# Row sums of twelve more attention pairs in groups of 16 rows, and another place for the squares of the weights

## The chip, the cores and the metric

The kernel runs on one core of a Trainium2 chip. The metric is device time in microseconds (us), the median of several executions; three executions before the change took 805.28, 805.90 and 806.34 us. The profile is of one more execution, taken by the hardware profiler.

## The reference

Three steps follow one another. The first is attention over 4 batches and 12 heads, 448 tokens, head size 64, with a soft cap on the scores:

```
scores = cap * tanh((q @ k.T / 8) / cap)
attn   = exp(scores - max);  attn = attn / sum(attn)
x      = attn @ v                                  # (4, 448, 768)
xk, xr = mu * x + (1 - mu) * x_prev                # two mixes with the token before
k      = relu(xk @ w_k);  y = sigmoid(xr @ w_r) * ((k * k) @ w_v)
theta  = y @ w_theta
u      = y + w_tok_r @ (y * cos(theta)) + w_tok_i @ (y * sin(theta))
out    = u + relu(u @ w_ch)
```

The weights arrive as 64-bit floats. The kernel turns them into float32 with shifts, finds a power-of-two scale from the sum of their squares, and splits each scaled value into two float16 parts, high and low; a large product is then three float16 matmuls.

## The kernel before, in words

**Layout.** Activations lie with features on the 128 partitions and the 448 tokens along the free side. Attention works on 24 pairs of heads, six to a batch.

**A pair.** `scores` (L633) makes the transposed scores of both heads in float32, four tiles of the array at a time (L653, L649). ScalarE applies tanh (L662) and exp (L666). Key rows 0 to 383 are three tiles `th`; the last 64 key rows are a half tile `tl`, in which the two halves of the partitions hold the two halves of the queries. VectorE adds the three full tiles into `z` (L739). Then the row sums, their reciprocals and the product with v follow, in one of two ways.

**`narrow` (L669), pairs 0 to 11.** The sums are 16 small float32 products into 32 array columns each (L676 with `z`, L680 with `tl`); sums of 16-row groups end up in eight groups on the partitions, 112 columns wide. VectorE takes the reciprocal of 128x112 (L687). Four float32 products (L692, `spread`) copy the reciprocals back over 128 partitions and 448 columns. The product with v (L698, L701) is copied out of PSUM with a scale (L703, recorded at L296 on ScalarE or L300 on VectorE), and VectorE multiplies it by the spread reciprocals, read from PSUM (L704).

**`wide` (L706), pairs 12 to 23 (`WIDE = 12`, L283).** Two additions first fold `tl` into `z` (L745). The sums are two products with a column of ones, broadcast to 64 array columns (L712), so they are on every partition at once. VectorE takes the reciprocal of 128x448 (L718), there is no spread, and one instruction scales the product with v (L724, L727) and multiplies by the reciprocals (L729).

**After a pair.** `attend` (L732) goes on to the two mixes with the token before (L751, L755), their float16 high part (L757) and low part (L758). Six finished pairs let a batch's products with w_k and w_r begin (`units`, L776, matmuls L783 to L785); they are laid between the matmuls of the next six pairs. After the last pair come the products with w_v (also L783 to L785), then the theta, token and channel products (L957 to L959, L987 to L989, L1009 to L1011).

**Weights.** `group` (L515) loads a block of raw 64-bit words into one of two buffers `w` (L380, L520, L530), rescales the exponent word (`rebase`, L451), and builds float32 in one of three buffers `f` with three VectorE steps (L461, L464, L467, the last one being `b3`). `squares` (L491) has ScalarE square `f` with a running sum (L495). The squares themselves are of no use and are written over the raw words, so `w` is in use until the square is done. A product with ones sums over partitions (L500), three tiny VectorE steps make the scale (`size`, L504), then the high part (L542) and the low part (L543) are written into the weight's tile. w_k takes its squares on the matrix engine (`grams`) and is not concerned. `tokens` (L863) does the same for the seven tiles of the two token matrices. The tile of w_theta and those of the token matrices exist once the last pair is done (`o_r2`, L852), that of w_ch once all w_k and w_r products are done (`o_l2`, L853).

**Order.** Each operation is declared with an engine, a duration, a rank and what it reads and writes. `Plan.order` (L149) runs the list through a small model with these durations and writes down one fixed order for each engine and for the DMA queue of SyncE. All engines then go through their list in that order, waiting where data is late. So a declared duration changes the order of every list after it.

Of the kernel before, what the change touches and what calls it, by code (L numbers as in the profile page):

```python
# [7 lines left out]
F32 = mybir.dt.float32  # L8
# [4 lines left out]
AF = mybir.ActivationFunctionType  # L13
ALU = mybir.AluOpType
# [4 lines left out]
B, H, S, D = 4, 12, 448, 64  # L19
# [5 lines left out]
SH = S // 2  # L25
# [5 lines left out]
KT = 7  # L31
# [217 lines left out]
def v1(n):  # L249
    return 0.17 + n / 940.0  # L250
# [6 lines left out]
def act(n):  # L257
    return 0.17 + n / 1150.0
# [19 lines left out]
def body(nc, tc, exact, qk, v, cap, mu_k, mu_r, w_k, w_v, w_r, w_th, w_tr, w_ti, w_ch, out):  # L278
    P = Plan()
    op = P.op  # L280
    ENG = {"ACT": nc.scalar, "DVE": nc.vector, "POOL": nc.gpsimd}
    SLOT = 7.9
    WIDE = 12  # L283
    WV0, WV1 = 190.0, 28.0
    WT0, WT1, WO0, WC0, WC1 = 1440.0, 10.0, 1510.0, 1660.0, 20.0
    K20, VM0, VM1 = 390.0, 1500.0, 100.0
# [21 lines left out]
    def tt(n, half=False):  # L308
        return {"POOL": pool(n) - 0.00021 * n * half, "DVE": v1(n)}
# [60 lines left out]
    def small(n=1):  # L370
        used[0] += n
        return Buf(tile=scal[:, used[0] - n:used[0]])
# [115 lines left out]
        op("PE", 0.3, rank, lambda: nc.tensor.matmul(ps.t[:, 0:1], unit[0:w].to_broadcast([w, 128]), d.t[0:w], start=True, stop=True), r=[d], w=[ps], name="bcast")  # L488
        return ps

    def squares(rank, parts, d):  # L491

        ps = Buf(c_ps)
        for a, (f, val, n, dead) in enumerate(parts):
            op("ACT", act(n) + 0.19, rank, lambda a=a, val=val, n=n, dead=dead: nc.scalar.activation(out=dead.t[:, 0:n], in_=val(), func=AF.Square, accum_out=d.t[:, a:a + 1]),  # L495
               r=[f] if f is not dead else [], w=[dead, (d, a)], name="norm")

        def total():
            for a in range(len(parts)):
                nc.tensor.matmul(ps.t[:, 0:1], unit.to_broadcast([128, 128]), d.t[:, a:a + 1], start=(a == 0), stop=(a == len(parts) - 1))  # L500
        op("PE", 0.2 + 0.1 * len(parts), rank, total, r=[d], w=[ps], name="bcast")
        return ps
# [12 lines left out]
    def group(rank, src, dst, m, inv, nb, after=(), early=False):  # L515

        sw, n = small(), 128 * nb
        vals, parts = [], []
        for a in range(len(dst)):
            w, f = Buf(w_s), Buf(f_s)  # L520
            vals.append(f)

            def half(i, w=w):
                return w.t[:, 0:2 * n].bitcast(U32).rearrange("p (n two) -> p n two", two=2)[:, :, i]

            def val(f=f):
                return f.t[:, 0:n]

            def ld(w=w, a=a):
                nc.sync.dma_start(out=w.t[:, 0:2 * n].bitcast(U32).rearrange("p (i n) -> p i n", i=nb),  # L530
                                  in_=src[n * a:n * a + n, 256 * m:256 * m + 256].rearrange("(i p) n -> p i n", p=128))
            op("DMA", 0.03 + n / 350, rank - 12, ld, w=[w], after=[o_open1], name="wld")
            bits(rank, lambda h=half: h(1), lambda h=half: h(0), val, val, n, w, f, f)
            parts.append((f, val, n, 128 if early else w))
        size(rank, grams(rank, [parts], small()) if early else squares(rank, parts, small(len(parts))), inv, m, sw)
        for a, f in enumerate(vals):
            def part(i, a=a):
                return dst[a].t[:, :, i, 128 * m:128 * m + 128]

            def val(f=f):  # L540
                return f.t[:, 0:n].rearrange("p (i n) -> p i n", i=nb)
            op({**cs(n), "DVE": (v1 if nb % 2 else v2)(n) + 0.06}, 0, rank, lambda e, val=val, part=part: copy(e, part(0), val(), sw.t), r=[f, sw], w=[(dst[a], (m, 0))], after=after, name="whi")  # L542
            grouped.append(op("DVE", v1(n) + 0.06, rank, lambda val=val, part=part: nc.vector.scalar_tensor_tensor(  # L543
                out=part(1), in0=val(), scalar=sw.t, in1=part(0), op0=ALU.mult, op1=ALU.subtract),
               r=[f, sw, (dst[a], (m, 0))], w=[(dst[a], (m, 1))], name="wlo"))
# [14 lines left out]
    for b in range(B):  # L560
        R = (2 * NP * b - 7.1) * SLOT if b else 3
        vb = v[NP * b:NP * b + NP].rearrange("g p n -> (g p n)").rearrange("(p n) -> p n", p=128)
        parts = []
        n = 2 * DM
        for c in range(2):
            t = Buf(w_s)
            op("DMA", 0.03 + n / 700, R - 10, lambda t=t, c=c, vb=vb: nc.sync.dma_start(out=t.t, in_=vb[:, c * n:(c + 1) * n]), w=[t], after=[o_open1], name="ldm")
            parts.append([(t, lambda t=t: t.t, n, 128)] if b == 0 else (t, lambda t=t: t.t, n, t))
        size(R, squares(R, parts, small(2)) if b else grams(R, parts, small()), small(), 0, sv[b])
        times(R, sv[b], qi, sx[b])  # L570
        inverse(R, sx[b], ix[b], 0.0, 2.0)
# [14 lines left out]
    last1 = []  # L586
# [79 lines left out]
            op("ACT", act(n * S) + 0.08, A + 3 + 1.8 * c, lambda th=th: nc.scalar.activation(out=th.t, in_=th.t, func=AF.Exp, scale=cap_t),  # L666
               w=[th], name="exp", table="exp")

    def narrow(A, x, sxb, th, vn, z, sp, rs, ps):  # L669

        def sums():

# [4 lines left out]
            for k in range(2):  # L677
                for h, i in ((0, 0), (0, 1), (1, 0), (1, 1)):
                    c = 32 * (2 * h + i)
                    nc.tensor.matmul(sp.t[c:c + 32, 0:SQ], ones[:, 1 + i, k], th[3].t[:, h, SQ * k:SQ * k + SQ], start=False, stop=(k == 1))  # L680
        op("PE", 0.74, A, sums, r=[z, th[3]], w=[sp], name="sums")

        def den():

# [5 lines left out]
        def spread():  # L690
            for i in range(4):
                nc.tensor.matmul(sp.t[:, SQ * i:SQ * i + SQ], live["row"][:, i].rearrange("p h d -> p (h d)"), rs.t, start=True, stop=True)  # L692
        op("PE", 0.8, A + 2, spread, r=[rs], w=[sp], name="spread")

        def av():
            for c in range(3):
# [6 lines left out]
        op({"ACT": act(S) + 0.09, "DVE": 0.7}, 0, A + 3, lambda e: copy(e, x.t[:, 1:S + 1], ps.t[:, 0:S], sxb.t), r=[ps, sxb], w=[x], name="avo")  # L703
        last1.append(op("DVE", v1(S), A + 6, lambda: nc.vector.tensor_tensor(out=x.t[:, 1:S + 1], in0=x.t[:, 1:S + 1], in1=sp.t[:, 0:S], op=ALU.mult), r=[sp], w=[x], name="norm"))  # L704

    def wide(A, x, sxb, th, vn, z, sp, ps):  # L706

        rs = lambda: x.t[:, 1:S + 1]

        def sums():  # L710
            for h in range(2):
                nc.tensor.matmul(sp.t[64 * h:64 * h + 64, 0:S], unit.to_broadcast([128, D]), z.t[:, h], start=True, stop=True, skip_group_check=True)  # L712
        op("PE", 0.74, A, sums, r=[z], w=[sp], name="sums")

        def den():
            if exact:
                nc.vector.tensor_scalar(out=rs(), in0=sp.t[:, 0:S], scalar1=1e-9, scalar2=None, op0=ALU.add)
            nc.vector.reciprocal(out=rs(), in_=rs() if exact else sp.t[:, 0:S])  # L718
        op("DVE", 2.95, A + 1, den, r=[sp], w=[x], name="den")

        def av():
            for c in range(3):
                for h in range(2):
                    nc.tensor.matmul(ps.t[64 * h:64 * h + 64, 0:S], vn.t[0][:, h, c], th[c].t[:, h], start=(c == 0), stop=False, skip_group_check=True)  # L724
            for i in range(2):
                for h in range(2):
                    nc.tensor.matmul(ps.t[64 * h:64 * h + 64, SH * i:SH * i + SH], vn.t[1][:, i, h], th[3].t[:, h], start=False, stop=True, skip_group_check=True)  # L727
        op("PE", 3.02, A + 0.5, av, r=[vn, *th], w=[ps], name="av")
        last1.append(op("DVE", v1(S) + 0.06, A + 4, lambda: nc.vector.scalar_tensor_tensor(  # L729
            out=x.t[:, 1:S + 1], in0=ps.t[:, 0:S], scalar=sxb.t, in1=rs(), op0=ALU.mult, op1=ALU.mult), r=[ps, sxb], w=[x], name="norm"))  # L730

    def attend(g):  # L732
        A = g * PAIR + 10
        th, vn = thb[g], vnb[g]
# [4 lines left out]
            op("DVE", v1(2 * S), A - 4 + i, lambda i=i: nc.vector.tensor_tensor(out=z.t, in0=th[0].t if i == 1 else z.t, in1=th[i].t, op=ALU.add),  # L739
               r=[th[0], th[1]] if i == 1 else [th[i]], w=[z], name="sum")  # L740

        if g >= WIDE:
            for i in range(2):
                p, q = slice(64 * i, 64 * i + 64), slice(SH * i, SH * i + SH)
                op(tt(S), 0, A - 1 + 0.5 * i, lambda e, p=p, q=q: e.tensor_tensor(out=z.t[p, :, q], in0=z.t[p, :, q], in1=th[3].t[p], op=ALU.add), r=[th[3]], w=[(z, i)], name="fold")  # L745
            wide(A, x, sx[b], th, vn, z, sp, ps)
        else:
            narrow(A, x, sx[b], th, vn, z, sp, rs, ps)
        R = A + 7
        d, t0 = Buf(mx_s), Buf(mx_s)  # L750
        op(tt(S), 0, R, lambda e: e.tensor_tensor(out=d.t, in0=x.t[:, 1:S + 1], in1=x.t[:, 0:S], op=ALU.subtract), r=[x], w=[d, (t0, "x")], name="mxd")  # L751
# [111 lines left out]
    def tokens(rank):  # L863
        fo = []
        for i in range(KT):
            raw, f = Buf(w_s), Buf(xf_s)
            parts = {3: ((w_tr, 384, 64, 0), (w_ti, 0, 64, 64))}.get(i, ((w_tr, 128 * i, 128, 0) if i < 3 else (w_ti, 128 * i - 448, 128, 0),))
            for src, r0, rows, p0 in parts:
                op("DMA", 0.03 + rows * S * 8 / 360e3, rank - 12, lambda src=src, r0=r0, rows=rows, p0=p0, raw=raw: nc.sync.dma_start(
                    out=raw.t[p0:p0 + rows, 0:2 * S].bitcast(U32), in_=src[r0:r0 + rows]), w=[(raw, p0)], after=[o_open1], name="wld")  # L870

            def half(j, raw=raw):
                return raw.t[:, 0:2 * S].bitcast(U32).rearrange("p (n two) -> p n two", two=2)[:, :, j]

            def fv(f=f):
                return f.t
            bits(rank, lambda h=half: h(1), lambda h=half: h(0), fv, fv, S, raw, f, f, [o_r2])
            fo.append((f, fv, S, raw))
        size(rank, squares(rank, fo, small(KT)), io, 0, so)
        tiny(rank, lambda: nc.vector.tensor_scalar(out=iw.t, in0=io.t, scalar1=2.0 ** 49, scalar2=None, op0=ALU.mult), r=[io], w=[iw])  # L880

        tiny(rank, lambda: nc.vector.tensor_scalar(out=tb.t, in0=io.t, scalar1=2.0 ** 70, scalar2=1.0, op0=ALU.mult, op1=ALU.add), r=[io], w=[tb])
# [210 lines left out]
```

## Time and profile before

| | |
|---|---|
| median of three executions | 805.9 us |
| the profiled execution | 805.84 us |
| its span, first to last instruction | 804.0 us |
| mean granted TensorE clock | 0.993 |
| busy: TensorE, VectorE, ScalarE, GpSimd | 96%, 70%, 55%, 12% |
| attention with wide sums | about 188 to 362 us |

PE is TensorE, DVE VectorE, ACT ScalarE, POOL GpSimd, SP SyncE; PEld is TensorE's weight load, and a q behind an engine's name its instruction queue, where DMAs are issued. A float32 matmul shows as two records. The recorded length of a matmul overlaps that of the next one; what a product takes of the engine's time is read from the starts of records that follow one another.

### The profile page before, as it was taken

How to read it: one execution, taken by the hardware profiler on the slowest of the kernel's cores; microseconds unless marked ns; L12 is line 12 of the kernel's file. 1: busy time of each engine (PE TensorE's matmuls, PEld its weight loads, DVE VectorE, ACT ScalarE, POOL GpSimd, SP SyncE). 2: the span in 40 equal slices, each digit the busy share in tenths (PEclk: the TensorE clock that was granted, in tenths of full speed). 3: DMA queues.
4: the chain of work that ended last, by engine and by line, in shares of the span. 5: the costliest groups of instructions: out<-in, count | busy, mean ns of one | idle time of the engine just before them, and what ended most of it. 6: DMA issues, size and time to landing. Idle time of an engine off the chain costs nothing.

```text
span 804.0 us, 12769 instructions
## 1 busy us (share of the span) xinstructions
PE 770.6 (96%) x4924; PEld 386.0 (48%) x4924; DVE 563.6 (70%) x1014; ACT 440.8 (55%) x677; POOL 92.6 (12%) x99
## 2 busy tenths in 40 slices
PE   5989999999999999998999889999999999999996
PEld 2445455454444444443555445555555555555553
DVE  2888897967778899879657768966856544645531
ACT  4889877878775875755526434355635333222201
POOL 1214403201130120101001000101201000000000
PEclk9999999999999999999999999999999999999999
DMA  8855455455343434225556866553535333324402
GB/s 258 257 173 181 158 180 191 138 171 184 113 136 99 139 92 157 97 75 172 176 191 221 296 193 203 185 152 84 123 60 136 82 92 92 90 65 98 99 28 73
DMA packets 116829, 114.76 MB, mean 143 GB/s; under 512 B 55820, under 2 KB 108824, under 8 KB 116760
## 3 DMA queue, kind: packets, MB, share of 16 engines
q1 hardware_dynamic: 116592, 113.86, 46.8%
q8 instruction: 40, 0.66, 0.3%
q14 instruction: 29, 0.24, 0.1%
q10 hardware_dynamic: 168, 0.01, 0.0%
HBM read 78.98 MB, written 23.86 MB: 128 GB/s over the span
## 4 chain that ended last, share of the span: by engine, by line
PE 87%; DMA 5%; DVE 4%; ACT 2%; issue 1%; SPq 1%; ACTq 0%; DVEq 0%
PE one L783 12%; PE one L784 11%; PE one L785 11%; PE big L653 7%; PE q L989 4%; PE q L987 4%; PE q L988 4%; PE one L724 4%; PE one L1010 3%; PE one L1009 3%; PE one L1011 3%; PE one L698 3%; PE q L957 2%; PE q L959 2%; PE q L958 2%; DMA w<-in_v 2%
## 5 line engine op out<-in xcount | busy, mean ns | idle before, releaser
L662 ACT ACTIVATE th<-big,tsc 128x896 f32<-128x896 f32 x72 | 70.1, 1002 | 22.6 <-PE big L653 22.4
L653 PE MATMUL big<-qk 64*64 64x448 f32 x576 | 67.8, 571 | 8.2 <-DMA qk<-in_qk 7.7
L783 PE MATMUL one<-k,wv 128*128 128x448 f16 x192 | 68.3, 356 | 6.2 <-DVE z L909 6.2
L666 ACT ACTIVATE th<-th,cap_t 128x896 f32<-128x896 f32 x72 | 73.0, 1039 | 0.0
L783 PE MATMUL one<-sl,wk 128*128 128x448 f16 x192 | 68.5, 357 | 2.4 <-ACT g L794 1.9
L784 PE MATMUL one<-sl,wk 128*128 128x448 f16 x192 | 68.2, 355 | 0.9 <-POOL sl L758 0.9
L784 PE MATMUL one<-k,wv 128*128 128x448 f16 x192 | 68.2, 355 | 0.0
L785 PE MATMUL one<-k,wv 128*128 128x448 f16 x192 | 68.1, 355 | 0.0
L785 PE MATMUL one<-sl,wk 128*128 128x448 f16 x192 | 68.1, 355 | 0.0
L989 PE MATMUL q<-wo,zt 128*128 128x448 f16 x168 | 59.2, 352 | 0.0
L987 PE MATMUL q<-wo,zt 128*128 128x448 f16 x168 | 59.2, 352 | 0.0
L988 PE MATMUL q<-wo,zt 128*128 128x448 f16 x168 | 59.2, 352 | 0.0
L1013 ACT ACTIVATE z<-one,scal 128x448 f32<-128x448 f32 x24 | 15.1, 627 | 71.9 <-PE one L1011 71.9
L783 PE MATMUL one<-sl,wr 128*128 128x448 f16 x144 | 50.9, 354 | 0.0
L785 PE MATMUL one<-sl,wr 128*128 128x448 f16 x144 | 50.7, 352 | 0.0
L784 PE MATMUL one<-sl,wr 128*128 128x448 f16 x144 | 50.7, 352 | 0.0
L973 DVE SCALAR_TENSOR_TENSOR cs<-xf,scal,cs 128x896 f32<-128x896 f32 x24 | 27.6, 1150 | 31.6 <-DMA xf<-xd 24.2
L718 DVE RECIPROCAL xt<-one 128x448 f32<-128x448 f32 x12 | 35.5, 2956 | 14.0 <-PE one L712 14.0
L758 POOL TENSOR_TENSOR sl<-mx,sl 128x448 f16<-128x448 f32 x24 | 29.5, 1230 | 119.2 <-ACT sl L294 100.6
L454 ACT ACTIVATE w<-w 128x768 f32<-128x768 f32 (+2 forms) x26 | 21.4, 823 | 35.0 <-DMA w<-in_w_ch 17.4
L1014 DVE TENSOR_TENSOR xf<-z,xf 128x448 f32<-128x448 f32 x24 | 15.0, 624 | 34.4 <-ACT z L1013 34.2
L991 DVE SCALAR_TENSOR_TENSOR xf<-q,scal,xf 128x448 f32<-128x448 f32 x24 | 16.4, 683 | 31.8 <-PE q L989 31.6
(191 smaller groups left out, 1739.5 us busy)
## 6 DMA issues: line engine op xcount, KB each, us to landing
qk<-in_qk SPq DMA_DIRECT2D x23, 448.0 KB, 3.8
kd<-g SPq DMA_DIRECT2D x32, 224.0 KB, 2.0
vn<-in_v SPq DMA_DIRECT2D x24, 256.0 KB, 2.7
w<-in_v SPq DMA_DIRECT2D x8, 768.0 KB, 6.2
w<-in_w_k SPq DMA_DIRECT2D x8, 768.0 KB, 5.1
w<-in_w_v SPq DMA_DIRECT2D x12, 512.0 KB, 4.4
zd<-tmp SPq DMA_DIRECT2D x24, 224.0 KB, 2.6
z<-zd SPq DMA_DIRECT2D x24, 224.0 KB, 2.9
```

The source lines that it names most:

```text
L653: nc.tensor.matmul(ps.t[o, h, 0:S], t.t[p, 1, 128 * c + 64 * i:128 * c + 64 * i + 64], t.t[p, 0], start=True, stop=True)
L662: op("ACT", act(n * S) + 0.08, A + 1 + 1.8 * c, lambda src=src, th=th: nc.scalar.activation(out=th.t, in_=src(), func=AF.Tanh, scale=tsc), ...
L666: op("ACT", act(n * S) + 0.08, A + 3 + 1.8 * c, lambda th=th: nc.scalar.activation(out=th.t, in_=th.t, func=AF.Exp, scale=cap_t), w=[th], ...
L718: nc.vector.reciprocal(out=rs(), in_=rs() if exact else sp.t[:, 0:S])
L724: nc.tensor.matmul(ps.t[64 * h:64 * h + 64, 0:S], vn.t[0][:, h, c], th[c].t[:, h], start=(c == 0), stop=False, skip_group_check=True)
L758: op(tt(S, True), 0, R + i, lambda e, t=t, hi=hi, lo=lo: e.tensor_tensor(out=lo.t, in0=t.t, in1=hi.t, op=ALU.subtract), r=[t, hi], w=[lo], ...
L783: nc.tensor.matmul(ps.t[:, 0:S], wh, xh(), start=(kk == 0), stop=False)
L784: nc.tensor.matmul(ps.t[:, 0:S], wh, xl(), start=False, stop=False)
L785: nc.tensor.matmul(ps.t[:, 0:S], wl, xh(), start=False, stop=(kk == len(xs) - 1))
L987: nc.tensor.matmul(o, z.t[:, 0, i], wo[i].t[:, 0], start=(i == 0), stop=False)
L988: nc.tensor.matmul(o, z.t[:, 1, i], wo[i].t[:, 0], start=False, stop=False)
L989: nc.tensor.matmul(o, z.t[:, 0, i], wo[i].t[:, 1], start=False, stop=(i == KT - 1))
```

## The change

All pairs take the way of `narrow`, now called `normal`; `wide` and its fold additions are gone. The declared durations of its sums and its spread are lowered, from 0.74 to 0.36 and from 0.8 to 0.47. The square of a weight block is written over the place of that block's own float16 parts instead of its raw words, and so must wait until that place exists.

```
-    WIDE = 12
...
-    def squares(rank, parts, d):
+    def squares(rank, parts, d, after=()):
...
-            op("ACT", ..., nc.scalar.activation(out=dead.t[:, 0:n], in_=val(), func=AF.Square, accum_out=d.t[:, a:a + 1]),
-               r=[f] if f is not dead else [], w=[dead, (d, a)], name="norm")
+            op("ACT", ..., nc.scalar.activation(out=place(), in_=val(), func=AF.Square, accum_out=d.t[:, a:a + 1]),
+               r=[f] if f not in dead else [], w=[*dead, (d, a)], after=after, name="norm")
...  (group)
-            parts.append((f, val, n, 128 if early else w))
-        size(rank, ... squares(rank, parts, small(len(parts))), inv, m, sw)
+            parts.append((f, val, n, 128) if early else (f, ..., n, [(dst[a], (m, 0)), (dst[a], (m, 1))],
+                          lambda a=a: dst[a].t[:, :, :, 128 * m:128 * m + 128].bitcast(F32)))
+        size(rank, ... squares(rank, parts, small(len(parts)), after), inv, m, sw)
...  (tokens)
-            fo.append((f, fv, S, raw))
+            fo.append((f, ..., S, [(wo[i], 0), (wo[i], 1)], lambda i=i: wo[i].t.bitcast(F32)))
...
-    def narrow(A, x, sxb, th, vn, z, sp, rs, ps):
+    def normal(A, x, sxb, th, vn, z, sp, rs, ps):
-        op("PE", 0.74, A, sums, r=[z, th[3]], w=[sp], name="sums")
+        op("PE", 0.36, A, sums, r=[z, th[3]], w=[sp], name="sums")
-        op("PE", 0.8, A + 2, spread, r=[rs], w=[sp], name="spread")
+        op("PE", 0.47, A + 2, spread, r=[rs], w=[sp], name="spread")
-    def wide(A, x, sxb, th, vn, z, sp, ps):
...
-        if g >= WIDE:
-            for i in range(2):
-                op(tt(S), ..., name="fold")
-            wide(A, x, sx[b], th, vn, z, sp, ps)
-        else:
-            narrow(A, x, sx[b], th, vn, z, sp, rs, ps)
+        normal(A, x, sx[b], th, vn, z, sp, rs, ps)
```

## Rows read from the trace of the kernel before

**Rows 1.** Busy time by stretch: span, then busy us of each engine, PEclk, DMA.

```profile
188.00:362.00 174.00, 173.08 (x1130) 76.31 (x1123) 145.19 (x217) 121.08 (x188) 24.62 (x21) 1.00 0.37 117
362.00:375.00 13.00, 10.12 (x47) 4.37 (x46) 11.49 (x17) 7.98 (x15) 3.59 (x3) 0.92 0.39 125
...
440.00:484.00 44.00, 36.41 (x193) 18.89 (x192) 31.55 (x73) 17.86 (x31) 2.86 (x4) 0.98 0.72 239
```

**Rows 2.** Waits of PE from 188 to 363 us: total, times, longest.

```profile
PE one L712 <- DVE xt L718: 0.9, 1, 0.9
```

**Rows 3.** Timeline of PE, a narrow pair: start, length, line.

```profile
114.96 0.59 PE L676 MATMUL one<-pz,ones 128*32 128x112 f32 x16
...
115.86 0.36 PE L783 MATMUL one<-sl,wk 128*128 128x448 f16 x1
...
118.52 0.35 PE L785 MATMUL one<-sl,wk 128*128 128x448 f16 x1
118.71 1.04 PE L692 MATMUL one<-rs,row 128*128 128x112 f32 x8
119.59 0.35 PE L783 MATMUL one<-sl,wk 128*128 128x448 f16 x1
```

**Rows 4.** Timeline of PE, the sums of a wide pair.

```profile
223.50 0.97 PE L712 MATMUL one<-pz,unit 128*64 128x448 f32 x4
224.40 0.36 PE L783 MATMUL one<-sl,wk 128*128 128x448 f16 x1
```

**Rows 5.** Chain that ended last, in time: start, us, what (two neighbourhoods).

```profile
26.07 1.07 PE one L692 x8
...
193.04 0.75 PE one L712 x4
```

**Rows 6.** Instructions by line and shape: busy us, mean ns, idle before and releaser.

```profile
L718 DVE RECIPROCAL xt<-one 128x448 f32<-128x448 f32 x12 | 35.5, 2956 | 14.0 <-PE one L712 14.0
L745 DVE TENSOR_TENSOR pz<-pz,tl 64x448 f32<-64x448 f32 x20 | 14.1, 706 | 0.5
L687 DVE RECIPROCAL rs<-one 128x112 f32<-128x112 f32 x12 | 10.2, 852 | 2.9 <-PE one L680 2.7
L729 DVE SCALAR_TENSOR_TENSOR xt<-one,scal,xt 128x448 f32<-128x448 f32 x12 | 8.2, 679 | 0.3 <-PE one L727 0.2
L704 DVE TENSOR_TENSOR xt<-xt,one 128x448 f32<-128x448 f32 x12 | 7.4, 621 | 7.0 <-PE one L692 7.0
L296 ACT ACTIVATE xt<-one,scal 128x448 f32<-128x448 f32 x9 | 5.7, 636 | 7.0 <-PE one L701 6.7
```

**Rows 7.** Waits of PE from 363 to 425 us.

```profile
PE one L783 <- ACT g L794: 1.8, 2, 1.6
PE one L784 <- POOL sl L758: 0.9, 1, 0.9
```

**Rows 8.** Waits of PE from 425 to 500 us.

```profile
PE one L783 <- DVE z L909: 6.2, 3, 2.9
```

**Rows 9.** Waits of SP's queue, whole span: total, times, longest.

```profile
SPq L530 <- ACT w L495: 43.9, 23, 4.4
```

**Rows 10.** Timeline around one load of w_ch: VectorE, ScalarE and SP.

```profile
462.59 0.95 DVE L467 SCALAR_TENSOR_TENSOR f<-w,f 128x768 uint32<-128x768 uint32 x1
...
467.08 0.83 ACT L495 ACTIVATE w<-f 128x768 f32<-128x768 f32 x1
...
467.51 0.43 SPq L950 DMA_DIRECT2D xf<-xd  x1
468.34 0.38 SPq L530 DMA_DIRECT2D w<-in_w_ch  x1
...
476.00 0.91 ACT L454 ACTIVATE w<-w 128x768 f32<-128x768 f32 x1 [5.74 <-DMA w<-in_w_ch]
```

**Rows 11.** w_theta: its low parts, and its first use (duration, first and last start).

```profile
L543 DVE SCALAR_TENSOR_TENSOR wt<-f,scal,wt x6: 1002/1008/1012, 368.9 to 400.4; 128x768 f16<-128x768 f32 x6
...
L957 PE MATMUL q<-xs,wt x96: 352/352/353, 468.9 to 734.3; 128*128 128x448 f16 x96
```

More of the change, by code (lines that the diff above doesn't have):

```diff
@@ L489, in grams @@
         return ps
-    def squares(rank, parts, d):
+    def squares(rank, parts, d, after=()):
         ps = Buf(c_ps)
-        for a, (f, val, n, dead) in enumerate(parts):
-            op("ACT", act(n) + 0.19, rank, lambda a=a, val=val, n=n, dead=dead: nc.scalar.activation(out=dead.t[:, 0:n], in_=val(), func=AF.Square, accum_out=d.t[:, a:a + 1]),
-               r=[f] if f is not dead else [], w=[dead, (d, a)], name="norm")
+        for a, (f, val, n, dead, place) in enumerate(parts):
+            op("ACT", act(n) + 0.19, rank, lambda a=a, val=val, place=place: nc.scalar.activation(out=place(), in_=val(), func=AF.Square, accum_out=d.t[:, a:a + 1]),
+               r=[f] if f not in dead else [], w=[*dead, (d, a)], after=after, name="norm")
         def total():
@@ L533, in group @@
             bits(rank, lambda h=half: h(1), lambda h=half: h(0), val, val, n, w, f, f)
-            parts.append((f, val, n, 128 if early else w))
-        size(rank, grams(rank, [parts], small()) if early else squares(rank, parts, small(len(parts))), inv, m, sw)
+            parts.append((f, val, n, 128) if early else (f, lambda val=val: val().rearrange("p (i t n) -> p i t n", i=nb, t=2), n, [(dst[a], (m, 0)), (dst[a], (m, 1))],
+                                                                     lambda a=a: dst[a].t[:, :, :, 128 * m:128 * m + 128].bitcast(F32)))
+        size(rank, grams(rank, [parts], small()) if early else squares(rank, parts, small(len(parts)), after), inv, m, sw)
         for a, f in enumerate(vals):
@@ L567, in body @@
             op("DMA", 0.03 + n / 700, R - 10, lambda t=t, c=c, vb=vb: nc.sync.dma_start(out=t.t, in_=vb[:, c * n:(c + 1) * n]), w=[t], after=[o_open1], name="ldm")
-            parts.append([(t, lambda t=t: t.t, n, 128)] if b == 0 else (t, lambda t=t: t.t, n, t))
+            parts.append([(t, lambda t=t: t.t, n, 128)] if b == 0 else (t, lambda t=t: t.t, n, [t], lambda t=t: t.t))
         size(R, squares(R, parts, small(2)) if b else grams(R, parts, small()), small(), 0, sv[b])
@@ L704, in narrow @@
         last1.append(op("DVE", v1(S), A + 6, lambda: nc.vector.tensor_tensor(out=x.t[:, 1:S + 1], in0=x.t[:, 1:S + 1], in1=sp.t[:, 0:S], op=ALU.mult), r=[sp], w=[x], name="norm"))
-    def wide(A, x, sxb, th, vn, z, sp, ps):
[L708 to L724, printed above, removed]
-            for i in range(2):
[L726 to L730, printed above, removed]
     def attend(g):
@@ L740, in attend @@
                r=[th[0], th[1]] if i == 1 else [th[i]], w=[z], name="sum")
-        if g >= WIDE:
-            for i in range(2):
-                p, q = slice(64 * i, 64 * i + 64), slice(SH * i, SH * i + SH)
-                op(tt(S), 0, A - 1 + 0.5 * i, lambda e, p=p, q=q: e.tensor_tensor(out=z.t[p, :, q], in0=z.t[p, :, q], in1=th[3].t[p], op=ALU.add), r=[th[3]], w=[(z, i)], name="fold")
-            wide(A, x, sx[b], th, vn, z, sp, ps)
-        else:
-            narrow(A, x, sx[b], th, vn, z, sp, rs, ps)
+        normal(A, x, sx[b], th, vn, z, sp, rs, ps)
         R = A + 7
@@ L877, in tokens @@
             bits(rank, lambda h=half: h(1), lambda h=half: h(0), fv, fv, S, raw, f, f, [o_r2])
-            fo.append((f, fv, S, raw))
-        size(rank, squares(rank, fo, small(KT)), io, 0, so)
+            fo.append((f, lambda f=f: f.t.rearrange("p (t n) -> p t n", t=2), S, [(wo[i], 0), (wo[i], 1)], lambda i=i: wo[i].t.bitcast(F32)))
+        size(rank, squares(rank, fo, small(KT), [o_r2]), io, 0, so)
         tiny(rank, lambda: nc.vector.tensor_scalar(out=iw.t, in0=io.t, scalar1=2.0 ** 49, scalar2=None, op0=ALU.mult), r=[io], w=[iw])
```

## The prediction

> **What bounds the kernel now.** I first read the busy time by stretch, to see which engine fills the stage that the change rewrites. In the stage with wide sums, 188 to 362 us, TensorE is busy 173.08 of 174 us at clock 1.00, VectorE 145.19 and ScalarE 121.08 [rows 1]. Busy time of overlapped matmuls can flatter, so the second view is TensorE's waits in that stage: one, of 0.9 us [rows 2]. The third is its timeline: from the product at 115.86 to the one at 118.52 are fourteen steps of 448 columns in 2.66 us, 0.19 us each [rows 3], which is 448 columns at 2.4 GHz, so nothing is left between them. TensorE bounds this stage, and what is added to its list there is added to the time, unless it fits into the few waits elsewhere. Those after the stage are at the join with the last batch, 362 to 375 us, where TensorE is idle 2.88 us at clock 0.92 [rows 1, 7], and in the w_v products, 440 to 484 us, where it waits 6.2 us for VectorE to empty a PSUM bank [rows 8].
>
> **Pairs 12 to 23, TensorE.** Removed: the wide sums. Start to next start they take 0.90 us between float16 products [rows 4], and 0.75 us where they follow the product with v, whose array shape they share [rows 5]; three of the twelve stand so in the timeline, hence a mean of (9 x 0.90 + 3 x 0.75) / 12 = 0.86 us. Added: the narrow sums, also 0.90 us (114.96 to 115.86) [rows 3]. They are 16 small products, but they stream as many columns as the wide ones, four at a time instead of two, and half of the steps are the `tl` rows, which the wide way had folded in on VectorE. Added as well: the spread, which the wide way doesn't have. It takes 0.88 us between float16 products (118.71 to 119.59) [rows 3] and 1.07 us between products of other array shapes [rows 5]. The stage is full of float16 products, so I take 0.90, near the first. A pair gains 0.90 + 0.90 - 0.86 = 0.94 us, twelve pairs 11.3 us. The bounds: 0.90 + 0.88 - 0.90 = 0.88 us, in all 10.6; and 0.90 + 1.07 - 0.75 = 1.22 us, in all 14.6. That the declared durations fall to 0.36 and 0.47 does not make the chip faster: the same instructions have the rows above.
>
> **Pairs 12 to 23, the other engines.** VectorE loses a 2.96 us reciprocal for one of 0.85, 14.1 us of fold additions, and 0.68 for 0.62 in the last product [rows 6]; over twelve pairs 25.3 + 14.1 + 0.7 = 40 us, less some 2 us for the three copies in twelve that VectorE made in the narrow pairs. ScalarE gets the other copies at 0.64 us [rows 6], some 6 us on 121 of 174. These I cost at nothing, and credit with little: TensorE covers both. Of the one wait of 0.9 us, for the long reciprocal [rows 2], all goes, as that reciprocal goes. The PSUM bank of the sums is now held through the spread to the last product, 0.90 + 0.85 + 0.90 + 0.62 = 3.3 us against 0.90 + 2.96 = 3.9 us before, so nothing is late for it; if waits lengthen that, the product with ones of a weight scale queues behind it on TensorE.
>
> **The join.** After the last pair's sums the chain was 2.96 + 0.68 us to a finished x; it becomes 0.85 + 0.90 + 0.62, so 1.3 us shorter [rows 3, 6]. Behind it stand casts and subtractions that also hold TensorE up (0.9 us for a GpSimd subtraction, 1.6 us for a ScalarE eviction [rows 7]); I credit 1.0 us. The bounds are nothing, and all 2.9 us of idle time with the 1.0 us that a clock of 0.92 costs over 13 us [rows 1].
>
> **Squares.** 23 loads wait for the square of an earlier block to free its raw words [rows 9]; now `b3` frees them. The case that matters is the load before the longest late eviction: `b3` ends at 463.54, the square starts at 467.08, the load is issued at 468.34 and lands for the rescale at 476.00 [rows 10]. But SP's list has an xf load just ahead, issued at 467.51 for 0.43 us, so with this list the gain is about 0.4 us; I take 0.4. It would be 4 us or more if the list puts the load further ahead, up to the whole 6.2 us of waits [rows 8]. Below nothing: a load issued earlier stands in SP's list ahead of loads that are wanted sooner; by the load's own 0.38 us of issue, shifted for each of 30 blocks and seven token tiles, that is 14 us of queue time in all, spread over 400 us and mostly off the path. The square writes as many bytes as before; its duration stays. It waits for its place: w_theta's blocks now start their squares after the last pair, but the last low part was written at 400.4 and first use is at 468.9 [rows 11], a cover of 68 us against a few squares of under 1 us. For w_ch the first square in the trace is behind the opening of its tile anyway.
>
> **Sum.** 805.84 (the profiled execution; 0.06 under the median of 805.9, and 1.84 over its span of 804.0) + 11.3 - 0.9 - 1.0 - 0.4 = 814.8 us.
>
> **A rule against this reading.** The trace says TensorE is full, by its waits and by the 0.19 us steps. The Trainium skill, Perfetto Trace Analysis, section Identifying the Most-Contended Engine, says that matmul busy share is a bad measure, and that weight-load busy share (with the share of peak arithmetic) should be read instead. By weight loads the stage stands at 76.31 of 174 us, 44% [rows 1], and VectorE at 83% would be the most contended; the sum would then follow VectorE, the second rival. The 0.19 us steps disagree with it in this stage.
>
> **Rivals.** *First, the late waits close.* Early-freed words and a shorter join could take all of them: 805.84 + 11.3 - 0.9 - 2.9 - 1.0 - 6.2 = 806.1 us. For it: these waits hang on in-order lists, and the lists are written anew. Against: a single list position decides each, and a transfer of some 7 us remains. Chance 0.13, around 805.5 to 809. *Second, faster: VectorE sets the pace of the wide stage,* and TensorE's matmuls stretch to fill it. Then 38 us of VectorE work leave and the 11.3 us fit into gaps. A full gain would be 805.84 - 38 = 768 us, a quarter of it 796; it decides from 11.3 us of hidden TensorE gaps on. For it: VectorE is busy 83% there, and waits 14.0 us for wide sums [rows 6]. Against: one wait of 0.9 us and steps with no gap. Chance 0.07. *Third, new waits.* The plan now declares a narrow pair 0.71 us lighter (0.74 + 0.8 less 0.36 + 0.47), against rows of 0.90 and 0.88, in all 24 pairs. VectorE's and ScalarE's lists may then hold instructions that wait for a TensorE which is behind the plan, with evictions queued behind them. One such wait costs 0.9 to 2.9 us as now [rows 2, 8]; three more of 2.9 make 823.5. Against: a plan in which TensorE is late mostly makes the others wait for it, not the reverse. Chance 0.18, from 819 up. That the change does not do what it says I see no room for.
>
> **How the numbers follow.** The forecast, chance 0.62, has its own range from 809 (10.6, with half of the late waits gone: 805.84 + 10.6 - 0.9 - 2 - 3.1 = 810.4, and a little more from the load) to 819.5 (14.6 with the 0.9 us alone gained). The range of 806 to 822 takes in most of the first rival and the lower part of the third. A measurement can tell about 0.2%, 1.6 us, from no change. Faster by more is the second rival, 0.07; within it lie those of the first under 807.4, 0.06; slower is the rest, 0.87.
>
> **What would show it.** TensorE's instructions grow by 12 x (32 + 8 - 4) = 432 records; L692 has 192 records and L676 and L680 384 each. Between about 188 and 373 us TensorE stays full with the stage some 11 us longer, while VectorE's busy time falls by near 38 us. L687 shows 24 times at 0.85 us. Waits of SP for L495 fall from 23 to few, replaced by waits for L467. The prediction is wrong if the spread takes less than 0.5 us from start to start among float16 products, if the stage with pairs 12 to 23 is not longer, or if TensorE's waits after 362 us change by more than 6 us in sum.

## The result, and the profile after

The changed kernel takes 813.12 us, the median of eight executions (809.86 to 815.58), against 805.82 us, the median of eight executions of the kernel before beside it: a ratio of 1.0084, with a 95% interval from 1.0062 to 1.0107. That is 7.3 us slower; the forecast was 9.0 us slower. The profiled execution took 813.44 us, 7.6 us more than the profiled one of before, over a span of 811.7 us.

In the file after, lines from L456 on stand one line earlier and those behind the removed function some 32 earlier: L495 is L494, L783 to L785 are L751 to L753, L794 is L762, L909 is L877.

Busy time of the profiled execution after, from the page:

```profile
PE 783.8 (97%) x5356; PEld 402.8 (50%) x5356; DVE 539.8 (67%) x1022; ACT 434.5 (54%) x660; POOL 85.0 (10%) x96
```

TensorE has 5356 matmul records where it had 4924: the 432 more that were worked out. VectorE's busy time fell by 23.8 us over the whole span (563.6 before), less than the 40 us of instructions that went, as the new order gave VectorE other operations. The stretches that answer to [rows 1], with the end of the stage moved to where the last pair now is (span, busy us of PE, PEld, DVE, ACT, POOL, then PEclk):

```profile
188.00:376.00 188.00, 188.00 (x1534) 93.60 (x1533) 122.91 (x225) 118.01 (x182) 12.40 (x13) 1.00 0.37 122
376.00:410.00 34.00, 31.52 (x166) 17.04 (x166) 28.38 (x60) 20.02 (x41) 4.22 (x4) 0.95 0.56 173
440.00:484.00 44.00, 40.53 (x211) 21.28 (x210) 34.67 (x85) 21.96 (x35) 4.11 (x5) 0.96 0.74 242
```

TensorE is full through the whole stage, while VectorE fell from 83% to 65% busy. Where TensorE still waits after the stage, which answers to [rows 7, 8]; the stage itself has no wait, so the one of [rows 2] is gone:

```profile
PE one L751 <- ACT g L762: 2.4, 2, 2.2
```

```profile
PE one L751 <- DVE z L877: 3.5, 3, 2.5
```

The first is the join, the second the w_v products. The narrow instructions by line and shape, which answer to [rows 6], and two groups of moved squares with one that still lies over its input (busy us, mean ns, idle before):

```profile
L692 PE MATMUL one<-rs,row 128*128 128x112 f32 x192 | 26.3, 280 | 1.0 <-DVE rs L687 1.0
L687 DVE RECIPROCAL rs<-one 128x112 f32<-128x112 f32 x24 | 20.5, 856 | 19.2 <-PE one L680 19.0
L704 DVE TENSOR_TENSOR xt<-xt,one 128x448 f32<-128x448 f32 x24 | 14.9, 620 | 21.5 <-PE one L692 21.4
...
L494 ACT ACTIVATE w<-w 128x1536 f32<-128x1536 f32 x6 | 8.9, 1476 | 0.6 <-DMA w<-in_v 0.6
L494 ACT ACTIVATE wr<-f 128x768 f32<-128x768 f32 x6 | 5.0, 842 | 4.8 <-DVE f L466 2.5 <-PE one L753 2.3
L494 ACT ACTIVATE wc<-f 128x768 f32<-128x768 f32 x6 | 5.0, 838 | 0.9 <-DVE wc L543 0.7
```

A square into the strided place of the float16 parts takes 838 to 842 ns; over the raw words, in the kernel before, the same shape took 836:

```profile
L495 ACT ACTIVATE w<-f 128x768 f32<-128x768 f32 x18 | 15.0, 836 | 9.3 <-issue 4.0 <-DVE f L467 3.9 <-DVE scal L511 1.4
```

So the place costs nothing in length. It does cost a wait: ScalarE stood idle for 2.3 us before the w_r squares until a w_r product was done (the row of `wr` above), and at 149.0 us a w_r product of TensorE waited 1.1 us, which the profile puts down to such a square. From 100 to 188 us this is TensorE's only wait in the changed kernel; the kernel before has no such wait:

```profile
PE one L751 <- ACT wr L494: 1.1, 1, 1.1
```

The waits of SP's queue, which answer to [rows 9], show that the loads are freed by `b3` now:

```profile
SPq L529 <- DVE f L466: 40.0, 18, 5.9
...
SPq L529 <- ACT w L494: 2.9, 2, 2.3
```

And the timeline of TensorE in a pair that was wide before, which answers to [rows 3, 4]:

```profile
304.70 0.59 PE L676 MATMUL one<-pz,ones 128*32 128x112 f32 x16
305.10 0.57 PE L680 MATMUL one<-tl,ones 128*32 128x112 f32 x16
305.60 0.36 PE L751 MATMUL one<-sl,wk 128*128 128x448 f16 x1
...
309.09 1.04 PE L692 MATMUL one<-rs,row 128*128 128x112 f32 x8
309.96 0.35 PE L751 MATMUL one<-sl,wk 128*128 128x448 f16 x1
```

Sums take 0.90 us from start to start and the spread 0.87, as in pairs 0 to 11.

**Two sums for each run.** To compare runs I split the time where the last pair's product with v starts, and end it where the last matmul starts (some 6 us without TensorE follow in every run). I take the float16 products out at 0.1886 us each, their usual step, since plans lay some of them on one side or the other. What is left ahead of that point is the attention's own TensorE time with all waits; behind it are the other small products, all waits and half-clock stretches. Of pairs 12 to 23, eleven wide sums lie ahead of that point in the kernel before, and twelve narrow sums with eleven spreads in the changed one. Before: the last pair starts at 358.7 us with 753 float16 products ahead, so 358.7 - 753 x 0.1886 = 216.7 us, and 24.2 us behind. After: 372.6 us with 765 ahead, so 228.3 us, and 20.3 us behind. The change costs 11.6 us ahead of the last pair and gives 3.9 back behind it: 7.7, as the spans differ.

### The profile page after: what moved, and what is told of

It reads as the page before. It is cut to its first block, busy times and chain, and to the rows that moved or that the text cites. A ratio compares the mean times of both kernels' runs of the same rounds, so it can differ in the third digit from the quotient of the medians.

```text
span 811.7 us, 13604 instructions
## 1 busy us (share of the span) xinstructions
PE 783.8 (97%) x5356; PEld 402.8 (50%) x5356; DVE 539.8 (67%) x1022; ACT 434.5 (54%) x660; POOL 85.0 (10%) x96
## 4 chain that ended last, share of the span: by engine, by line
PE 84%; DMA 6%; DVE 5%; ACT 3%; issue 1%; ACTq 0%; DVEq 0%; SPq 0%
PE one L751 11%; PE one L752 10%; PE one L753 10%; PE big L653 6%; PE one L698 6%; PE q L957 4%; PE q L955 4%; PE q L956 4%; PE one L977 3%; PE one L979 3%; PE one L978 3%; PE one L692 2%; PE q L925 2%; PE q L927 2%; PE q L926 2%; PE one L701 2%
## 5 line engine op out<-in xcount | busy, mean ns | idle before, releaser
L751 PE MATMUL one<-k,wv 128*128 128x448 f16 x192 | 68.3, 356 | 3.6 <-DVE z L877 3.5
L751 PE MATMUL one<-sl,wk 128*128 128x448 f16 x192 | 68.6, 357 | 2.4 <-ACT g L762 2.4
L753 PE MATMUL one<-sl,wk 128*128 128x448 f16 x192 | 68.3, 356 | 0.4 <-DVE wk L543 0.4
L753 PE MATMUL one<-k,wv 128*128 128x448 f16 x192 | 68.2, 355 | 0.0
L698 PE MATMUL one<-th,vn 128*64 128x448 f32 x288 | 59.4, 548 | 0.0
L751 PE MATMUL one<-sl,wr 128*128 128x448 f16 x144 | 50.9, 354 | 1.2 <-ACT wr L494 1.1
L753 PE MATMUL one<-sl,wr 128*128 128x448 f16 x144 | 50.7, 352 | 0.0
L977 PE MATMUL one<-w_u,wc 128*128 128x448 f16 x108 | 38.1, 352 | 0.0
```

What stands on the lines that cost most here:

```text
L751: nc.tensor.matmul(ps.t[:, 0:S], wh, xh(), start=(kk == 0), stop=False)
L753: nc.tensor.matmul(ps.t[:, 0:S], wl, xh(), start=False, stop=(kk == len(xs) - 1))
L977: nc.tensor.matmul(ps.t[:, 0:S], wh, u.t[:, 0], start=(kk == 0), stop=False)
```

## The experiments

Every kernel ran in three rounds beside the kernel before, whose own median in the three jobs was 805.3 to 805.5 us. It varied from 802.3 to 809.1 us over these executions, more than in the three shown at first, so a difference of 2 or 3 us in one profile proves nothing by itself. The ratio is from all executions, but the two sums are from the one that was profiled. It lies within 1.2 us of its kernel's median, with three exceptions: 7.1 us above it for the pairs narrow with old durations and old squares (826.1 us), 3.0 above for the last pair narrow, and 1.6 below for the squares moved with folds on VectorE.

| kernel | median us | ratio to before, 95% interval | ahead of the last pair | behind |
|---|---|---|---|---|
| before | 805.8 | | 216.7 | 24.2 |
| changed | 813.1 | 1.0062 to 1.0107 | 228.3 | 20.3 |
| wide sums twice | 810.5 | 1.0051 to 1.0117 | 225.2 | 20.0 |
| no long reciprocal | 801.9 | 0.9942 to 0.9973 | 215.8 | 20.5 |
| squares moved only | 809.9 | 1.0040 to 1.0095 | 223.6 | 22.4 |
| pairs narrow, squares old | 813.9 | 1.0098 to 1.0159 | 227.7 | 20.5 |
| changed, old durations | 808.1 | 1.0014 to 1.0046 | 227.2 | 17.5 |
| pairs narrow, old durations, squares old | 819.0 | 1.0115 to 1.0197 | 231.6 | 29.4 |
| small durations only | 807.8 | 1.0011 to 1.0048 | 217.2 | 26.5 |
| squares moved, folds on VectorE | 803.5 | 0.9961 to 0.9994 | 217.7 | 19.3 |
| folds on VectorE only | 806.7 | 1.0000 to 1.0048 | 217.8 | 24.2 |
| last pair narrow | 805.4 | 0.9977 to 1.0010 | 218.3 | 25.5 |
| squares moved, folds on VectorE, wide from 9 | 804.5 | 0.9962 to 1.0006 | 215.2 | 25.8 |
| the same, wide from 5 | 811.0 | 1.0037 to 1.0090 | 226.1 | 20.9 |

### Is TensorE full? The wide sums twice

```
-            for h in range(2):
+            for h in [0, 1] * 2:
                 nc.tensor.matmul(sp.t[64 * h:64 * h + 64, 0:S], unit..., z.t[:, h], ...)
```

> The kernel before with the wide sums of pairs 12 to 23 issued twice and nothing else changed; declared durations and so every engine's list are those of before. Theory (TensorE is full in this stage, so each us added to its list is added to the time): 12 x 0.75 us to 12 x 0.90 us, 9 to 10.8 us more, 815 to 817 us, and the waits of TensorE after 362 us as before, within 2 us in sum. Rival (VectorE sets the pace and TensorE has hidden gaps): less than 3 us more, under 809 us.

The doubled sums in TensorE's timeline of that run:

```profile
225.52 1.72 PE L712 MATMUL one<-pz,unit 128*64 128x448 f32 x8
227.18 0.36 PE L783 MATMUL one<-sl,wk 128*128 128x448 f16 x1
```

They take 1.66 us from start to start, 0.76 more than in [rows 4], with every engine's list as before. Ahead of the last pair 8.5 us came on top. Of these 0.5 stand there ahead of pair 12 already; the eleven doubled sums make 8.4, and the wait for the long reciprocal fell from 0.9 to 0.6: nothing was hidden in the stage. But the median rose by 5.2 us only (interval 4.1 to 9.4), to 810.5 us, between the two ranges that I expected; the profile has 4.2 us less behind the last pair. So the theory holds for the stage, and fails in its second half, that the late waits stay.

### Does VectorE set the pace? No long reciprocal

```
-            nc.vector.reciprocal(out=rs(), in_=rs() if exact else sp.t[:, 0:S])
+            nc.vector.tensor_scalar(out=rs(), in0=rs() if exact else sp.t[:, 0:S], scalar1=4.3e-6, scalar2=None, op0=ALU.mult)
```

> The kernel before, with the same lists, in which the 128x448 reciprocal of pairs 12 to 23 is a multiplication by a constant: the normalization of these pairs is not computed. It takes VectorE work of 12 x (2.96 - 0.6 to 0.7) = 27 us out of that stage and nothing from TensorE. Theory (TensorE is full): 0.9 us of its waits goes, and up to 1 us at the join, so 804 to 805.5 us. Rival (VectorE sets the pace of the stage, busy 83%): 10 to 27 us less, 779 to 796 us.

The instruction that took its place, and the stage in that run:

```profile
L718 DVE TENSOR_SCALAR xt<-one 128x448 f32<-128x448 f32 x12 | 7.5, 622 | 16.5 <-PE one L712 16.5
```

```profile
188.00:362.00 174.00, 174.00 (x1134) 76.42 (x1128) 120.97 (x217) 121.59 (x190) 23.68 (x21) 1.00 0.36 118
```

VectorE lost 28 us of work, and ahead of the last pair the time fell by 0.9 us, the one wait of [rows 2]. VectorE does not set the pace there, although it was busy for 83% of the stage. The whole gain, 3.4 us to 801.9, is more than the theory expected and far less than the rival. The rest of it came behind the last pair, 3.7 us less in the profile: up to 425 us TensorE's waits shrank to 1.6 us from 3.1 (those of [rows 7] and one of 0.4 for a cast), and the granted clock from 362 to 375 us was 1.00 instead of 0.92. There the last reciprocal was in the chain.

### The squares alone, and why they were slow

The squares, group and tokens parts of the change on the kernel before:

> The kernel before with the squares moved to the place of the float16 parts, and the pairs as they were. TensorE's work is that of before. Theory (the moved squares free the raw words earlier, only the waits after 362 us and in the first 100 us can change, by a new order): 798 to 808 us, most likely 803, since part of the 6.2 us of waits in the w_v products goes. Rival (the moved squares cost by themselves, as they wait for their place and hold ScalarE's list): 808 to 815 us.

The rival's number came out, 809.9 us, but not by its mechanism. The loss is ahead of the last pair, 6.9 us, and 5.7 us of it is at two waits for folds, of 2.2 and 1.9 us, the longer with a slow product behind it. GpSimd's two folds in a row, TensorE's wait for them, and that product in the timeline (one line later in this file):

```profile
252.36 3.03 POOL L746 TENSOR_TENSOR pz<-pz,tl 64x448 f32<-64x448 f32 x2
...
255.44 0.97 PE L713 MATMUL one<-pz,unit 128*64 128x448 f32 x4 [2.19 <-POOL pz L746]
...
256.24 4.12 PE L725 MATMUL one<-th,vn 128*64 128x448 f32 x12
```

The twelve records of the product with v take 4.12 us instead of 2.48: after the wait the granted clock was 0.55, near the lower of its two levels (1.2 and 2.4 GHz). After the other wait, at 295.85 us, it stayed at 1.00. The stretches behind the two waits:

```profile
256.24:260.00 3.76, 3.76 (x14) 1.34 (x12) 3.54 (x2) 0.00 (x0) 0.00 (x0) 0.55 0.02 4
296.00:300.00 4.00, 4.00 (x22) 1.74 (x21) 4.00 (x5) 3.45 (x6) 0.71 (x1) 1.00 0.36 106
```

The new plan had put the folds on GpSimd, 1.5 us each, at a place where TensorE needs them. The test is to let VectorE alone do them:

```
-                op(tt(S), 0, A - 1 + 0.5 * i, lambda e, p=p, q=q: e.tensor_tensor(...), name="fold")
+                op({"DVE": v1(S)}, 0, A - 1 + 0.5 * i, lambda p=p, q=q, e=nc.vector: e.tensor_tensor(...), name="fold")
```

> The kernel with the moved squares alone (809.9 us), in which the fold additions of the wide pairs may only go to VectorE. In that run TensorE waited 2.2 us for two folds of 1.5 us on GpSimd and 1.9 us for one on VectorE, and the product behind ran at half clock. Theory (the loss of the moved squares is where a new order put folds, not the squares): 803 to 807 us. Rival (the moved squares cost by themselves): 808.5 to 812 us.

803.5 us: the 6.9 us ahead of the last pair are gone but 1.0, and no wait of TensorE is left from 188 to 366 us. So the loss was the folds' place, not a cost that the squares always bring, and this version is 0.2% faster than the kernel before (interval 0.9961 to 0.9994). The same restriction without the squares:

> The kernel before with its folds on VectorE alone, squares as before. Theory (the gain of the run with moved squares and folds on VectorE is the moved squares, which free the raw words): 805 to 807 us, as in the kernel before TensorE waits for no fold. Rival (the gain is from the folds): 802 to 804 us.

806.7 us, as the theory has it, with 24.2 us behind as before. Behind the last pair the moved squares have 19.3 us; this is where words freed earlier would show. The intervals of the two versions against the kernel before do not overlap, but the two also have different orders, and an order alone moved other kernels here by as much. So I call the squares' gain likely, not shown.

### The pairs alone, and the declared durations

The changed kernel with the squares of before:

> The changed kernel with the squares written over the raw words as before: all pairs narrow, durations 0.36 and 0.47. Theory (the pairs cost 11 to 12.5 us of TensorE work, the waits elsewhere go by the order): 813 to 822 us, and TensorE's products in the attention of pairs 12 to 23 end 11 to 15 us later than before. Rival (the loss is from the squares or from waits that the order sets, not from the pairs): 804 to 809 us.

813.9 us, 8.6 more, and 11.0 us more ahead of the last pair, both as the theory has it. The durations then: the changed kernel with 0.74 and 0.8,

> The changed kernel with the declared durations of before (sums 0.74, spread 0.8), so a plan that knows TensorE's load better; the instructions are those of the changed kernel. Theory (the loss is TensorE work, 12 us, less what late waits give back): 811 to 817 us, like the changed kernel's 813. Rival (the too small durations misplace the lists and cost several us): 803 to 809 us.

the kernel before with 0.36 and 0.47,

> The kernel before with the two smaller declared durations in its twelve narrow pairs and nothing else. The work of every engine is that of before. Theory (declared durations alone decide only which waits fall where): 802 to 809 us. Rival (they misplace the lists): 809 to 815 us, with TensorE waits before 188 us or at the join grown by the difference.

and all pairs narrow with the old durations and old squares.

> The kernel before with all pairs narrow, the old squares and the old declared durations: the narrow work alone. Theory (TensorE gets 12 us of work, of which the waits after 362 us give some 3 to 5 back, as when the wide sums were issued twice): 809 to 814 us, the last pair's products starting 9.5 to 12 us later than in the kernel before. Rival (with a plan that knows the load, the narrow pairs cost nothing, as the long reciprocals and folds go): 803 to 807 us.

Two of these three expectations missed. The changed kernel with the old durations took 808.1 us, in the rival's range and 3 us under the theory's; the pairs narrow with old durations and old squares took 819.0 us, 5 us above the theory's. The small durations alone gave 807.8 us, as expected.

The four kernels with all pairs narrow have 10.5, 11.0, 11.6 and 14.9 us more than before ahead of the last pair, whatever the plan; the last of them has 4.5 us more ahead of pair 3 already, so some 10 behind that. That is the TensorE work. Their totals run from 808.1 to 819.0 us, and the difference is in waits and slow stretches: 17.5 us behind in the best, 29.4 in the worst, whose profile is of its slowest execution. TensorE's waits from 188 to 500 us in the best one, the changed kernel with the old durations:

```profile
PE one L751 <- DVE z L877: 2.6, 3, 1.2
PE one L751 <- DVE scal L508: 2.1, 1, 2.1
PE one L499 <- ACT wo L494: 0.4, 2, 0.2
PE one L751 <- ACT g L762: 0.2, 1, 0.2
```

The join, 2.4 us of eviction waits in the changed kernel, is down to 0.2. The small durations cost 5.0 us here (813.1 against 808.1) and 2.3 us in the kernel before (807.8 against 805.5), but with the old squares the medians lie the other way, 813.9 against 819.0, of four executions each, with intervals that overlap. So these runs show no rule that a duration declared too small is slow; it gives another order, with its own late waits.

### Towards a better version

The last pair narrow and the others wide, so that the short reciprocal is in the join's chain:

```
-        z, sp, rs, ps = Buf(pz_s), Buf(c_ps), Buf(rs_s), Buf(a_ps)
+        z, sp, rs, ps = Buf(pz_s), Buf(c_ps), None if WIDE <= g < NG - 1 else Buf(rs_s), Buf(a_ps)
...
-        if g >= WIDE:
+        if WIDE <= g < NG - 1:
```

> The kernel before with pair 23 narrow and pairs 12 to 22 wide. TensorE gets 0.9 us more work; the reciprocal behind the last sums falls from 2.96 to 0.85 us. Taking that reciprocal away in all wide pairs gave 3.4 us, nearly all at the join. Theory (the join waits for the last pair's reciprocal): 802 to 804.5 us, excess time at the join 1.5 to 3 us where it was 5.1. Rival (the join waits for the casts and subtractions behind): 806 to 808 us.

No change, 805.4 us (0.9977 to 1.0010), between the two ranges. The eviction at the join waits as long as before:

```profile
PE one L783 <- ACT g L794: 1.8, 2, 1.6
PE one L712 <- DVE xt L718: 0.9, 1, 0.9
PE one L784 <- POOL sl L758: 0.3, 1, 0.3
```

The wait for the GpSimd subtraction shrank from 0.9 to 0.3 us, the one of 0.4 for a cast is gone, and the granted clock from 364 to 396 us was 1.00 instead of 0.95. So part of the chain behind the last reciprocal is not the reciprocal's, and in this profile, of an execution 3 us above the median, what was won there was lost in other places behind.

The other way, more wide pairs, from the best version:

> The version with moved squares and folds on VectorE (803.5 us), wide from pair 9 on. Three pairs lose 0.94 us of TensorE work each and VectorE gets 3 x 3.3 us = 10 us in the stage from 100 to 188 us, where it is busy 74.7 of 88 us and TensorE 87.7. Theory (TensorE still bounds that stage, VectorE at 84.7 of 88 just fits): 800 to 802.5 us. Rival (VectorE becomes the bound there): 804 to 808 us.

> The same version, wide from pair 5 on. Seven pairs lose 0.94 us of TensorE work each, 6.6 us, and VectorE gets 7 x 3.3 = 23 us, 20 of it in the stage from 100 to 188 us, which makes 94 to 95 us of work for a stage of 88 us less 6. Theory (VectorE bounds that stage then, and the narrow pairs are right there): 806 to 815 us, with TensorE waits for VectorE in that stage. Rival (TensorE bounds it all the way): 796 to 799 us.

From pair 9 on: 2.5 us less ahead of the last pair, near the 2.8 of three pairs, and 804.5 us in all, the rival's number. VectorE does not bound that stage, though: TensorE is busy 87.05 of the 88 us, and what was won ahead is lost behind the last pair, where the profile has 6.5 us more. The medians, 804.5 and 803.5, are not told apart. From pair 5 on it turns over, to 811.0 us as the theory has it, with 8.4 us more ahead of the last pair than the version wide from 12. In that run the stretches from 80 to 100 and from 100 to 188 us, and TensorE's three longest waits in the first of them:

```profile
80.00:100.00 20.00, 14.59 (x120) 6.24 (x119) 19.42 (x33) 16.56 (x24) 6.16 (x7) 1.00 0.43 142
100.00:188.00 88.00, 86.25 (x544) 37.44 (x543) 79.74 (x122) 63.39 (x94) 22.22 (x19) 0.98 0.43 147
```

```profile
PE one L500 <- DVE pz L746: 1.6, 1, 1.6
PE big L654 <- ACT th L663: 1.5, 1, 1.5
PE one L713 <- DVE scal L507: 1.4, 1, 1.4
```

The loss is earlier than I expected. From 80 to 100 us VectorE is busy 19.42 of 20 us and TensorE only 14.59; it waits for VectorE's additions (`pz`) and its scale steps (`scal`), and for banks that ScalarE empties (`th`). In the version wide from 12 the same 20 us have 17.75 and 19.30. Another 5.1 us of TensorE's waits lie from 188 to 367 us, where that version has none. From 100 to 188 us VectorE is not full, 79.7 of 88 us. So VectorE does bound where the first of these wide pairs fall, beside the first weights that it builds, and there the narrow way is worth its TensorE time. This is one plan of each.

## Why the prediction was right

**The bound.** TensorE is full in the wide stage: doubled sums cost their whole length there, and 28 us less for VectorE gave 0.9. The second rival, by which VectorE sets the pace, is out for this stage. The start-to-start step of 0.19 us told it rightly.

The rule that went with that rival (the Trainium skill, Perfetto Trace Analysis, section Identifying the Most-Contended Engine) names two measures of how close TensorE is to its peak, and only one was read here: weight loads were 44% busy in a stage that had no room. As a sign of room for more work, that share misled here; the share of peak arithmetic was not worked out.

**The TensorE term.** Forecast 11.3 us for twelve pairs. From start to start in the two traces, the twelve new sums take 0.91 us each and the twelve new spreads 0.88 to 0.98, 0.92 on average, as five of them stand beside products of other array shapes; the removed wide sums took 0.88. That is 0.95 us a pair, 11.4 us, so each part of the term was right, within the bounds given. The 0.75 us for wide sums behind the product with v is a step of the chain; from start to start those three take 0.85, and the product ahead of them is 0.10 shorter, so the sum stands.

**What the term left out.** Ahead of the last pair the sum asks for 10.3 us more (11.3, less the 0.9 us wait, with one spread against one wide sum behind that point); measured are 11.6. The wait of a w_r product for a moved square, 1.1 us, is near the difference, in one profile of each. The prediction priced the squares' wait for their place for w_theta and w_ch, and had nothing for w_r. In the two runs with moved squares and the pairs as before, TensorE has no such wait from 100 to 188 us, so this one too hangs on the order.

**The join.** Forecast 1.0 us gained; the waits fell from 3.1 to 2.4 us (those of [rows 7] and 0.4 for a cast, against the one line shown above), an eviction by ScalarE still the longest. About right, for one profile; the granted clock over 34 us from the last pair on was 0.95 in both.

**The squares.** Forecast 0.4 us gained, with up to 6.2 if the list put the load further ahead. TensorE's waits in the w_v products fell from 6.2 to 3.5 us, and one of 1.4 us for the sum of a square, which the kernel before has there as well, is gone. In sum TensorE's waits behind 362 us fell from 10.7 to 5.9 us, by 4.8: less than the 6 us that were to prove the prediction wrong. How much of it the squares made, and how much a later TensorE finds ready, stays open: doubled sums, with every list and the squares as before, also had 4.2 us less behind the last pair.

**The total.** It came out nearer than its parts. The profiles differ by 11.6 us ahead of the last pair, 1.3 more than the sum asks for, and by 3.9 us given back behind it, 2.5 more than the 1.4 that it credits there. That these two misses oppose each other is luck, and part of why the 9.0 us of the forecast lie so near the 7.3 of the medians.

**The other signs.** L687 stands 24 times at 0.86 us; SP's waits for a square fell from 23 to 2, and 18 for `b3` took their place. From 188 to 373 us TensorE is busy 185.0 of 185 us, and VectorE's busy time fell by 34 us (154.7 to 120.6), near the 38 expected.

**The third rival,** new waits from too small durations, is not borne out as a rule: with the old durations the changed kernel is 5.0 us faster, but with the old squares no loss from the small ones shows. The changed kernel had a new wait of 1.1 us, for a square, and fewer late ones. The forecast treated the order as a bound on the late waits, and that is what the runs show; it could not have told which way they go.

## What to carry to other kernels

Price an edit on the engine whose starts follow one another without a gap, by start-to-start time of the same instructions elsewhere in the trace, and credit the engines behind it with almost nothing: 40 us of VectorE instructions were removed here and the kernel got slower. An engine's busy share over a long stage can hide a short stretch where it is full: look at the stretch in which the other engine waits. Where a planner writes the order, a change of work and a change of order come together; several plans of the same work (here 808 to 819 us) tell the two apart, and a single plan does not. Give a narrow and a wide form of the same step to the stages by which engine is full in each.

## What the runs showed of the hardware

A wait of TensorE can cost more than its length: in the run with moved squares a wait of 2.2 us was followed by a product that took 4.12 us instead of 2.48, at a granted clock of 0.55. It need not: a wait of 1.9 us in the same run was followed by a clock of 1.00. The two forms of the row sums cost TensorE the same among float16 products: 16 float32 products of 112 columns took 0.90 us [rows 3], two of 448 columns 0.90 [rows 4]. Executions of one and the same kernel spread more than expected, the kernel before from 802.3 to 809.1 us and the changed one from 809.9 to 815.6; intervals, not single times, decide at this size.
